# A new order of steps for a fused attention and gated-convolution kernel on one core

## The chip, the cores and the metric

The kernel runs on one core of one Trainium2 chip. The metric is device time in microseconds, from the first to the last instruction on the core as the host's runs report it; 2% is the smallest change that such runs are read for. A profiled execution gives the trace: each engine's instructions with their start, their length and what they waited for. The engines are PE (matrix products), DVE and ACT (elementwise work and copies out of the product banks), POOL and SP (here mostly issuing DMAs).

## The reference

Attention with 4 batches, 8 heads, 768 positions and 64 columns a head, in which each query sees 8 global keys and a local window of 96, with a bias that falls with distance. Its output, heads side by side (768 x 512), goes through a gated convolution over the sequence:

```python
scores = scale * np.matmul(q, k.transpose(0, 1, 3, 2))
is_global = pos[None, :] < int(n_global)
is_local = (rel >= 0) & (rel < int(n_local))
dist = np.where(is_global & ~is_local, float(n_local), np.abs(rel).astype(np.float32))
bias = -slopes[:, None, None] * dist[None, :, :]
scores = np.where(is_global | is_local, scores + bias[None, :, :, :], -1000000000.0)
a = softmax(scores)              # in the reference: max, exp, sum, written out
x = heads_side_by_side(a @ v)    # 4 x 768 x 512
proj = x @ w_proj                # 512 x 1536
x1, x2, x3 = (proj[..., :D], proj[..., D:2 * D], proj[..., 2 * D:])
X2 = np.fft.rfft(x2, n=S, axis=1)
H = np.fft.rfft(filter_fft, n=S, axis=0)[None, :, :]
x2_conv = np.fft.irfft(X2 * H, n=S, axis=1)
return ((x1 * x2_conv * x3) @ w_out).astype(np.float32)
```

All inputs and the output are float32 in DRAM; the kernel computes in float16 with float32 sums.

## The kernel before

The work is cut into 949 steps. A step is one to some sixteen instructions of one engine: a load, a group of score products into a bank, an exponential out of it, a product with the values, a division, a turn, a projection, a transform, an eviction, a store. Each batch has two stages. *Attention*: q and k are loaded, turned so that the 64 columns of a head lie along the partitions, multiplied (line 811, `scores`) key block by key block (seven blocks of 120 keys, with the 8 global keys ahead in each), exponentiated on ACT (line 823), masked on DVE (line 835), multiplied with v (lines 861 and 866) and divided by their sum (`xn`, line 885 in one DVE instruction for all heads, or line 889 in one small ACT instruction a head). *Convolution* (`conv`): x is turned (`xT`, line 913), projected with the 512 x 1536 weights (lines 988 to 993: gates; line 1049: the part that is convolved), transformed by products with cosine and sine tables after butterfly sums, multiplied with the filter's spectrum (lines 1216 to 1234), transformed back (lines 1136 to 1141), gated (lines 1191 to 1196) and multiplied with `w_out` (line 1100); an eviction into a buffer `ot` (line 318, one of six buffers) and a store of 256 KB (line 1107) follow. The attention of a batch overlaps the convolution of the one before.

The front does work of its own: tables of angles (a product of one-row tiles, lines 504 to 519), their sines by ACT, distances and masks (`dg`, `mask`), and idle products.

**What sets the order.** `ORDER` is a string of one word a step: `204P1` is step 204 on PE with product bank 1, `191A` step 191 on ACT. The letters are P (PE), A (ACT), V (DVE), G (POOL) and S (SP). `schedule` turns the string into the program, and each engine executes its words in this order; a step that can run on ACT or DVE goes where its letter says, and each step's inputs and buffers are guarded by semaphores between engines. The word `i1b0` is an idle product: one 128 x 512 product on a tile of zeros into bank 0, of which nothing is used (`busy`, line 310).

**How data comes in.** POOL issues 80 loads (line 330), DRAM to SBUF with a cast to float16, in the order of their words. A load waits until the one eight before it has landed. The first batch's q and k come as pairs of heads (`96x2x512`, four of each; one of each is loaded by SP), everything else by blocks of rows (`120x8x64` for k and v, `128x8x64` for q), the filter in one load of 768 KB (`g`), the projection's weights in slices (`w`). SP issues the copies of the global rows of k and v within SBUF (`kn<-kn`, `vn<-vn`), all stores, and, for the fourth batch alone, the turns by the crossbar (DMA_TRANSPOSE: q and k at line 773, x at line 900). The other batches are turned by products with the identity.

Of the kernel before, what the change touches and what calls it, by code (L numbers as in the profile page):

```python
# [43 lines left out]
204P1 22A 217V 38G 209P2 23V 26G 205A 219P0 39V 62V 63V i1b3 220A 52G 108P3 206V 210A 66P4 194A 207V 109A i1b5 27G  # L44
i1b5 211V 106P5 221V 42G 67V i1b1 i1b1 94P1 43G 212V 114P67 208A 110V 222V 92P4 213A 40G 95V i1b2 218A 111P23 223A
107A i1b0 41G 96V 64P0 93V i1b1 259G 115P 53V 224V 103P45 68V 65V 46G 195A 104P 112P 116A 80P1 199V 257G 9V 105A 81V
100P67 i1b0 i1b0 113A 101P 82V 225V 97P01 102A 6V 72P23 98P 232V 31A 73P 86P67 260G 99A 33S 117P45 226V 198V 74A 233V
78P0 118P 79A 75P23 234V 44G 76P 119A 32V 87P 235V 83P01 45G 77A i1b4 236V 69P45 256G 88A 70P 237V 84P 89P23 71A 258G
90P 238V 125P67 85A i1b4 227V 48G 126V 135P45 127V 91A 47G 120P01 136V 252P67 121V 267G 137V 130P23 253A 122V 241P4
254A 272G 138P5 131V 123P0 132V 249P67 266G 139V 352P1 251A 152P23 353V 273G 242A 133P7 250A 153V 157P45 268G 154V  # L50
124A 128P6 350P0 265G 158V 129A 155P1 159V 348P2 197A 354A 156A 49G 246P6 349V 160P4 351A 50G 244P5 134V 247A 161V
360P01 362P23 203V 271G 182V 361A 239P4 181V 140P67 274G 240A 175V 363A 174V 261G 143P01 177V 141A 202V 51G 245A
355P67 144V 275G 357P23 356A 377P5 375P4 176V 460G 358A 378V 414P6 165P01 184V 376A 264G 183V 415V 379A 277G 255V
380P45 385P67 381A 146P23 200V 185V 386A 178V 464G 142V 412P4 145V 186A 416P5 179V 162P67 476G 262S 180V 147A 417V
263S 413A 471G 148V 187V 387P23 418A 163A 149P45 359V 388A 243V 188V 289P6 270G 150A 189V 419P23 269G 290A 382P45 201V
279P7 151V 383A 389V 478G i1b6 420A 365P45 276G 281P6 166A 366V 367V 463G 280A 421P23 364V 426P01 282A 424P45 293P7
480G 422A 384V 283P6 425A 294V 461G 299P23 427A 167V 370P45 423V 477G 368P7 284A 171P01 369A 371V 472G 372V 300A
390P67 428V 462G 172A 395P45 164V 285P23 248A 469G 396V 173V 228P0 286A 391V 397V 291P1 470G 301V 229A 555P2 230A 392V
465G 434P45 292A 302V 231A 429P67 556A 468G 287V 168P01 430V 678G 557A 435V 431V 475G 551P2 436V 169A 373P3 553P6 664G
393P7 552A 374V 619P4 554V 398P5 295P01 394V 481G 620A 399V 580P2 288V 296A 563P45 663G 467S 565P67 581V 578P3 566A  # L60
466S 437P0 297V 667G 617P2 564A 170V 432P1 438V 686G 400P67 298V 618A 579V 682G 433A 309P2 567V 401A 681G 560P45
558P01 307P3 452V 310A 403P67 679G 561A 451V 685G 559A 305P2 402V 311P4 308A 453V 677G 303P5 404A 317P0 621V 454V
315P3 479G 306A 615P1 562V 406P67 318A 316A 670G 312A 616V 304A 455V 573P23 666G 407A 313P1 574V 405V 627P45 582A 456V
278G 314A 482P0 575V 628A 683G 408V 588P67 457V 483A 622P23 590P45 492P1 623A 474G 320V 319V 591A 409P23 665G 458V
493A 321V 674G 589A 459V 502P01 568P45 473G 322V 668S 503A 494P6 569V 323V 684G 410A 496P7 570V 495A 675G 324V 583P23
497A 624P45 592V 439P01 625A 676G 584A 504V 680G 585P45 626V 629P67 440A 571P2 484P3 673G 630A 411V 325V 498P01 586A
442P67 631V 762S 485A 326V 499A 486P3 760S 587V 443A 598P01 637P45 487A 599V 327V 761S 572A 445P67 600A 638V 639V 758S
488P23 441V 593P45 501V 489A 576P0 759S 333P1 328V 446A 632P23 594V 500V 334A 671S 595A 448P67 490V 669S 505V 784S
633V 336P1 444V 577A 634V 449A 640P4 601P0 491V 337A 768P23 596P5 641V 783S 769A 512P6 602V 508P7 597V 513A 765P01
509V 770P23 763P45 766A 786S 329V 635P6 506P7 771A 518P0 636V 510P1 785S 507V 764A 514P6 654V 606P23 511A 822S 519A  # L70
655V 515A 516P1 345P0 450V 517A 447V 821S 607A 772V 520P1 346A 794P67 787P23 608V 792P45 338S 521A 767V 342P0 793A
819S 656V 330P1 788A 522V 820S 778P45 343A 523V 603P23 331A 657V 795A 779V 658V 773P01 604A 612P67 332S 774V 780V 524A
672S 775V 339P4 613A 796V 828P01 340A 789P67 659V 825P23 605V 790A 341S 609P45 525V 829A 660V 526V 642P67 826A 781S
791V 4A 610A 823P23 776S 614V 830P01 3A 824A 611V 645P45 527V 831A 661V 782S 802P23 528V 643A 648P01 803V 529V 646A
335S 777S 804A 651P45 662V 644V 827V 797P67 649A 806S 700P2 798V 832V 799A 833P01 805S 647V 531V 689P3 701A 800S 702P6
834V 530V 690A 691P7 835V 703A 801S 652A 704P23 532V 838P01 692A 837S 705A 653V 693P67 839V 687P4 840V 694A 836S 698P5
706V 688A 695V 536P6 842S 699A 707V 709P45 696V 537A 533P7 841S 710A 708V 810P01 697V 534A 347S 711V 548P7 712V 811A
855V 721P6 719P0 722A 723P1 725P4 549A 856V 715P5 717P6 716A 727P2 550S 713P7 726A 545P3 344S 858V 720A 714A 857V
539P0 728A 718A 859V 542P2 724A 540A 860V 729V 875P1 546A 861V 547S 846P67 730V 862V 731A 864P3 863V 876A 732V 879P0
543A 865A 733V 544S 877P1 880A 538S 812V 734V 541S 886P23 878A 735V 868P0 887A 650V 738V 881P45 869A 866P1 882A 888V  # L80
816P23 736V 867A 883V 870P01 817A 807P45 889V 871A 884V 813P23 818V 808A 885V 847A 873V 911P4 892P5 809V 912A 896P0
872V 907P1 897A 849P67 893A 874V 908A 737V 814A 894P1 890P0 895A 905P5 739V 909P4 891A 843P23 906A 898V 910A 899V 914V
900A 852P45 913V 848V 915A 901V 815V 916V 749P0 853A 902V 917V 755P1 903V 750A 918V 844A 904V 751S 752P4 919V 535S
756A 854V 845V 740P5 933V 757S 850A 935V 746P1 753A 851V 934V 743P0 754S 747A 936V 741A 748S 943P1 920V 744A 742S
937P5 922V 944A 945S 921V 940P4 938A 745S 923V 939S 930P5 941V 942S 924P1 2A 931A 927P0 932S 925V 946P5 926S 928A 947A
929S 948S
"""


# [1292 lines left out]
```

## Time and profile before

| | us |
|---|---|
| median of three runs | 167.62 |
| the three runs | 166.46, 167.62, 171.16 |
| profiled execution, span from first to last instruction | 166.3 |
| PE busy, share | 157.9, 95% |
| DVE busy, share | 151.4, 91% |
| ACT busy, share | 148.2, 89% |
| POOL busy, share | 73.8, 44% |
| last step: product, eviction, store, end | from 162.25 |

Of the profiled execution only the span is given as its time; it lies 0.2 us under the fastest of the three runs. Three engines are busy for about nine tenths of the span, and they hand work to each other through eight product banks and a few buffers, so no single engine's sum tells the time: a wait on one shows as a gap on the next. Read the busy shares together with what ended each engine's idle time, and by stage: the front (up to some 20 us), the stretch in which loads still come in (to about 91 us), the stretch with turns by the crossbar, and the end.

### The profile page before, as it was taken

Reading aid. Unit: us, or ns where it says so; the run is one execution under the profiler, and the core shown is the slowest. Engines: PE = TensorE matmul, PEld = TensorE weight load, DVE = VectorE, ACT = ScalarE, POOL = GpSimd, SP = SyncE. Lnnn points to the kernel's source line nnn. Section 1 sums busy time; section 2 is a strip of 40 time slices with the busy share of each in tenths; the row PEclk is TensorE's granted clock in tenths of the full one; section 3 lists DMA queues with packets and bytes.
Section 4 is the critical chain, followed back from the end, with each engine's and each line's share of the span. In section 5 each row is a group of like instructions: output and inputs, shape, how many; then the busy total and the mean of one; then the engine's idle time right before and its main releaser. Section 6 shows DMA issues by size and latency. Waiting matters only on the chain.

```text
span 166.3 us, 4460 instructions
## 1 busy us (share of the span) xinstructions
PE 157.9 (95%) x1735; PEld 98.2 (59%) x1735; DVE 151.4 (91%) x348; ACT 148.2 (89%) x268; POOL 73.8 (44%) x94
## 2 busy tenths in 40 slices
PE   6999998999999999999999999999999699999991
PEld 2356566856536687765566685566555454585440
DVE  6898699899979999999999999999999979999960
ACT  3999995998999979999999999999997579998972
POOL 7896399999699979999730000000000000000000
PEclk9999999999999999999999999999999999999999
DMA  5999999999999999999999656423133135000696
GB/s 151 146 138 194 160 161 153 170 170 176 175 162 149 152 148 125 137 145 139 159 152 144 122 97 155 85 79 110 40 73 112 68 129 189 0 4 0 252 348 221
DMA packets 90365, 22.84 MB, mean 137 GB/s; under 512 B 81504, under 2 KB 87016, under 8 KB 90344
## 3 DMA queue, kind: packets, MB, share of 16 engines
q0 software_dynamic: 74880, 12.46, 100.9%
q1 hardware_dynamic: 15464, 10.10, 22.2%
q8 instruction: 13, 0.21, 0.5%
q14 instruction: 8, 0.07, 0.1%
HBM read 25.69 MB, written 6.29 MB: 192 GB/s over the span
## 4 chain that ended last, share of the span: by engine, by line
PE 50%; DMA 16%; DVE 15%; POOL 13%; issue 2%; SPq 1%; ACT 1%; ACTq 0%; POOLq 0%; DVEq 0%
PE bank L988 10%; PE bank L1100 10%; PE bank L1049 7%; DMA g<-in_moe_filter_fft_dram 6%; PE bank L990 5%; POOL kn L330 4%; DMA vn<-in_v_dram 4%; POOL qn L330 4%; DMA vn<-vn 3%; PE bank L811 3%; DVE xn L885 2%; DMA out_dram<-ot 2%; PE bank L861 2%; DVE E L835 2%; PE bank L866 2%
## 5 line engine op out<-in xcount | busy, mean ns | idle before, releaser
L823 ACT ACTIVATE E<-bank 128x864 f16<-128x864 f32 x48 | 40.5, 909 | 1.2 <-PE bank L811 1.1
L988 PE MATMUL bank<-xT,w 128*128 128x384 f16 x192 | 34.7, 326 | 0.0
L318 ACT ACTIVATE x<-bank 128x768 f16<-128x768 f32 (+2 forms) x31 | 25.5, 830 | 2.4 <-PE bank L988 1.0
L330 POOL DMA_DIRECT2D vn<-in_v_dram x28 | 25.6, 923 | 2.2 <-DMA w<-in_moe_w_proj_dram 1.6
L988 PEld LDWEIGHTS <-w 128*128 128x128 f16 x192 | 17.7, 98 | 11.1 <-issue 0.3
L1100 PE MATMUL bank<-wo,y 128*128 128x512 f16 (+1 forms) x100 | 22.5, 370 | 0.0
L330 POOL DMA_DIRECT2D kn<-in_k_dram x24 | 21.8, 910 | 1.5 <-DMA wo<-in_moe_w_out_dram 1.0
L330 POOL DMA_DIRECT2D qn<-in_q_dram x21 | 18.4, 881 | 5.7 <-DMA g<-in_moe_filter_fft_dram 4.2
L835 DVE TENSOR_TENSOR E<-E,mask 128x1728 f16<-128x1728 f16 x18 | 18.8, 1048 | 0.0
L318 ACT ACTIVATE ot<-bank 128x512 f32<-128x512 f32 (+1 forms) x23 | 12.9, 599 | 3.5 <-PE bank L1100 1.8
L885 DVE TENSOR_TENSOR xn<-bank,rc 128x512 f16<-128x512 f32 (+1 forms) x20 | 15.5, 789 | 0.3
L861 PEld LDWEIGHTS <-E 128*128 128x128 f16 x224 | 14.1, 97 | 2.8 <-DVE E L835 0.7
L1049 PE MATMUL bank<-w,xab 128*128 128x512 f16 x64 | 15.6, 379 | 0.0
L861 PE MATMUL bank<-vn,E 128*128 128x65 f16 x224 | 15.3, 193 | 0.2 <-DMA vn<-vn 0.2
L1100 PEld LDWEIGHTS <-y 128*128 128x128 f16 x100 | 9.5, 98 | 10.0 <-issue 0.3
L866 PE MATMUL bank<-vn,E 128*128 128x65 f16 x192 | 15.1, 193 | 0.0
L314 ACT CAST ab<-bank 128x512 f16<-128x512 f32 x23 | 13.7, 607 | 0.7 <-PE bank L1049 0.6
L866 PEld LDWEIGHTS <-E 128*128 128x128 f16 x192 | 13.2, 97 | 0.9
L811 PE MATMUL bank<-QT,KT 64*128 64x216 f16 (+2 forms) x224 | 13.3, 241 | 0.4 <-DVE pp L1229 0.4
L314 ACT CAST eo<-bank 128x384 f16<-128x384 f32 x30 | 12.9, 523 | 0.5 <-PE bank L1141 0.5
L314 ACT CAST X<-bank 128x1024 f16<-128x1024 f32 x12 | 12.2, 1032 | 0.0
L811 PEld LDWEIGHTS <-KT 64*128 64x128 f16 x224 | 7.9, 94 | 6.6 <-issue 5.2
(187 smaller groups left out, 363.0 us busy)
## 6 DMA issues: line engine op xcount, KB each, us to landing
out_dram<-ot SPq DMA_DIRECT2D x23, 256.0 KB
vn<-in_v_dram POOLq DMA_DIRECT2D x28, 120.0 KB, 6.1
kn<-in_k_dram POOLq DMA_DIRECT2D x21, 120.0 KB, 6.4
qn<-in_q_dram POOLq DMA_DIRECT2D x18, 128.0 KB, 6.1
w<-in_moe_w_proj_dram POOLq DMA_DIRECT2D x4, 256.0 KB, 6.8
g<-in_moe_filter_fft_dram POOLq DMA_DIRECT2D x1, 768.0 KB, 10.6
kn<-in_k_dram POOLq DMA_DIRECT2D x3, 192.0 KB, 4.3
qn<-in_q_dram POOLq DMA_DIRECT2D x3, 192.0 KB, 5.0
```

The costliest lines, as they stand in the source:

```text
L314: {"A": nc.scalar.copy, "V": nc.vector.tensor_copy, "G": nc.gpsimd.tensor_copy}[e](out, in_)
L318: self.nc.scalar.mul(out, in_, c)
L330: return self.g.op(eng, 0.57 + 0.00035 * nbytes[0] if eng == "G" else 0.5, lambda _: e.dma_start(dst, src), w=w, r=r, nbytes=nbytes, name= ...
L811: nc.tensor.matmul(bs[hh].f32()[:, off:off + w], self.KT[hs, hp, P * m:P * m + P], self.QT[hs, hp, KL * m:KL * m + w], start=(off == 0 and ...
L823: g.op("A", act(864), lambda _: nc.scalar.activation(eo, bs[0].two()[:, :, 0:432].rearrange("p h (m w) -> p h m w", m=2), Act.Exp, scale=s ...
L835: g.op("V", dve(1728, 2), lambda _: nc.vector.tensor_mul(ep, ep, mk), r=[("mask", h) for h in range(hs.start, hs.stop)] + ([("mask0", hp - ...
L861: nc.tensor.matmul(o[:, n, hh], ef[:, at:at + P], vt[:, t, 2 * hp + hh, 0:D + 1], start=first, stop=(t == 0), skip_group_check=True)
L866: nc.tensor.matmul(o[:, n, hh], ef[:, at:at + P], vt[:, t - 1, 2 * hp + hh, 0:D + 1], start=False, stop=True, skip_group_check=True)
L885: nc.vector.tensor_mul(to, o[:, :, :, 0:D], rc.to_broadcast([P, 2, 2 * nt, D]))
L988: nc.tensor.matmul(bk.f32()[:, 0:h], w, self.xT[:, c, lo:lo + h], **kw)
L1049: nc.tensor.matmul(bk.f32(), src[:, c], w[:, c, DM:2 * DM], start=(c == 0), stop=(c == 3))
L1100: nc.tensor.matmul(bk.f32()[:, 0:n], y[:, c, P * t:P * t + P], self.wo[:, c, ns], start=(c == 0), stop=(c == 3))
```

## The change

The string `ORDER` is another one; nothing else in the file differs. It holds the same 949 steps, 18 idle products instead of 26, other banks, and for 48 steps the other one of ACT and DVE. It is one line shorter, so line numbers in the new file are smaller by one. Its first lines, and one from the middle:

```diff
-0V 34G 18S 30S i1b0 15V i1b0 21S 5G 35V i1b0 60V i1b0 59V 57V 10G 55V 7V i1b0 14V i1b0 24G 1V 56V 191A 8V i1b0 17V 61A
-28G 190A i1b0 12A 20V i1b0 36V i1b0 19A 54V 58V 37G 214P0 13V 193A i1b1 29G 11V 215A i1b1 16V 192A i1b1 196A 25G 216V
...
+18S 0V 15V 36V 6V 7V 14A 5G 21S 12A 25G 8V i1b0 i1b0 i1b0 i1b0 219P0 220A 221V 204P1 222V 24G 205A 28G 209P2 210A 211V
+10G 61V 27G 214P3 215A 29G 16V 30S 26G 34G 52G 206V 207V 223A 216V 23A i1b4 i1b4 i1b4 i1b4 i1b4 64P0 i1b4 i1b4 66P1
...
+782S 341S 831A 651P23 660V 833P67 829A 648P45 347S 524V 776S 644V 525V 647V 806S 652A 526V 800S 661V 834V 687P2 835A
```

**PE, front.** Before, ten idle products stand ahead of the first product of the angle tables (steps 214, 204, 209, 219), and the other sixteen follow one to three at a time, up to the values of the second batch. Now four stand ahead of the four angle steps and five behind them, then come the first turns of q and k (steps 64 and 66) with two idle products between them, and the last seven follow ahead of step 111.

**POOL, front.** POOL's queue from its first own instructions to the first loads of v: `dg` is the distance table, `eo` a spare buffer with the rows for the angle tables, `ident` the identity, `g_85` the filter, `96x2x512` a pair of heads of the first batch. Before:

```order
L549 IOTA dg 128x216
L551 AFFINE_SELECT dg<-dg 128x216 x2
L403 IOTA eo 1x512
L405 IOTA eo 1x128
masks.py:197 MEMSET ident 128x128
masks.py:199 AFFINE_SELECT ident<-ident 128x128
L330 DMA kn<-in_k_dram 96x2x512 x2
L568 AFFINE_SELECT eo<-eo 8x120 x2
L330 DMA qn<-in_q_dram 96x2x512 x2
L571 AFFINE_SELECT tail<-tail 128x1
L330 DMA kn<-in_k_dram 96x2x512
L330 DMA g_85<-in_moe_filter_fft_dram 128x6x512
```

Now:

```order
L402 IOTA eo 1x512
L404 IOTA eo 1x128
L329 DMA qn<-in_q_dram 96x2x512
L329 DMA kn<-in_k_dram 96x2x512 x2
masks.py:197 MEMSET ident 128x128
masks.py:199 AFFINE_SELECT ident<-ident 128x128
L329 DMA qn<-in_q_dram 96x2x512 x2
L329 DMA kn<-in_k_dram 96x2x512
L548 IOTA dg 128x216
L550 AFFINE_SELECT dg<-dg 128x216 x2
L329 DMA g_85<-in_moe_filter_fft_dram 128x6x512
```

The distance table moved from first place to just ahead of the filter, three loads moved ahead of the identity, and all six pair loads are ahead of the filter, which is the seventh load and not the sixth. Behind it, blocks of q and k of the second batch now come ahead of the first v blocks, and the weight slices are later: the one from column 1280 is the 31st load and was the 29th.

**ACT, front.** From ACT's first instructions: `mask` is the exponential of the distance table, `E` and `y` belong to the angle tables, `ab` and `identb` are casts. Before:

```order
L314 CAST identb<-ident 128x128
L612 ACTIVATE mask<-dg 128x216
L447 COPY E<-eo 128x2x6x32
L448 ACTIVATE E<-eo 128x2x80
L314 CAST ab_87<-ot 96x512
```

Now:

```order
L446 COPY E<-eo 128x2x6x32
L447 ACTIVATE E<-eo 128x2x80
L460 ACTIVATE y<-bank_104 128x256
L460 ACTIVATE y<-bank_104 128x512
L460 ACTIVATE y<-bank_105 128x256 x2
L474 ACT_TABLE_LOAD
L474 ACTIVATE p_81<-y 128x256
```

The work on the angle tables moved ahead of the masks; six of the eight masks now stand between the first batch's score exponentials or behind them, where seven stood ahead of these.

**SP, from the end of q's and k's turns.** SP's queue, stores (`out_dram<-ot`) and turns of x (`xT<-xn`, with two or three blocks each). Before:

```order
L1107 DMA out_dram<-ot 128x512
L900 DMA_TRANSPOSE xT<-xn_70 128x2x128
L900 DMA_TRANSPOSE xT<-xn_69 128x2x128
L900 DMA_TRANSPOSE xT<-xn_70 128x2x128
L1107 DMA out_dram<-ot 128x512
L900 DMA_TRANSPOSE xT<-xn_69 128x2x128
L900 DMA_TRANSPOSE xT<-xn_70 128x2x128 x2
L900 DMA_TRANSPOSE xT<-xn_69 128x2x128 x2
L900 DMA_TRANSPOSE xT<-xn_69 128x3x128 x2
L900 DMA_TRANSPOSE xT<-xn_70 128x3x128 x2
L1107 DMA out_dram<-ot 128x512 x13
```

Now:

```order
L1106 DMA out_dram<-ot 128x512
L899 DMA_TRANSPOSE xT<-xn_69 128x2x128
L899 DMA_TRANSPOSE xT<-xn_70 128x2x128
L1106 DMA out_dram<-ot 128x512 x2
L899 DMA_TRANSPOSE xT<-xn_69 128x2x128
L899 DMA_TRANSPOSE xT<-xn_70 128x2x128
L899 DMA_TRANSPOSE xT<-xn_69 128x2x128 x2
L899 DMA_TRANSPOSE xT<-xn_70 128x2x128
L899 DMA_TRANSPOSE xT<-xn_69 128x3x128 x2
L899 DMA_TRANSPOSE xT<-xn_70 128x3x128 x2
L1106 DMA out_dram<-ot 128x512 x14
```

Two stores (steps 341 and 347) now stand together ahead of the last nine turns; before, one (step 335) stood there, and step 347 was the first behind the turns. Steps 332 and 335 are now behind them. Farther ahead in SP's queue, the thirteen turns of the fourth batch's q and k start with step 759, right behind the last score products of the third batch (step 588), and stand closer together; before, they started with step 762, some ten microseconds of PE's work later.

More of the change, by code (lines that the diff above doesn't have):

```diff
@@ L47 @@
[L47 to L81, printed above, removed]
@@ new lines @@
+104P 198V 83P45 274G 49G 105A 232V 9V 99A 233V 234V 226V 50G 117P01 84P 118P 235V 227V 85A 86P23 87P 88A 75P67 76P
+348P4 236V 261G 119A 125P23 350P5 89P01 237V 77A 351A 349V 352P4 238V 270G 196A 126V 127V 199V 264G 120P67 121V 197A
+353V 135P23 239P5 90P 240A 136V 122V 244P4 91A 462G 130P67 241P5 354V 242A 137V 357P01 157P23 131V 224V 123P5 358A
+245V 464G 51G 132V 138P4 152P67 195A 194A 158V 159V 355P01 269G 460G 153V 124A 200V 139A 133P5 160P2 201V 128P4 1V
+134A 463G 246P3 377P5 154V 356A 161V 129A 362P67 360P01 378V 361A 471G 182V 181V 247A 184V 17V 263S 363A 155P2 461G
@@ new lines @@
+575V 311P0 307P1 316A 309P4 590P67 588P23 312A 308A 676G 453V 591A 313P5 409P01 759S 405V 629P67 454V 455V 587V 589A
+624P23 314A 758S 492P5 310A 303P4 625A 410A 406P23 456V 304A 576P4 493A 682G 482P5 407A 562V 457V 442P23 411V 458V
+762S 577A 568P01 626V 592V 459V 675G 681G 483A 569V 630A 631V 443A 502P45 503A 598P67 683G 599V 760S 484P2 444V 637P45
+680G 570A 486P3 278G 786S 600V 571P0 632P67 485A 319V 408V 761S 487A 593P23 638V 320V 572A 639V 488P01 321A 439P45
+594V 633V 489A 785S 595V 634V 763P23 322V 440A 783S 764A 768P01 504V 784S 769A 448P67 449A 494P2 640P3 673G 765P01
@@ L87 @@
+854V 901V 849P23 749P0 916V 902V 917V 746P1 753A 903V 918V 756A 904V 850A 919V 851V 740P2 935V 750A 747A 933V 754S
+936V 934V 743P3 946P1 920V 757S 741A 922V 943P2 947V 940P0 751S 937P1 921V 748S 742S 744A 745S 944A 945S 948S 941A
+938A 942S 2A 939S 923V 924P0 925V 927P1 928V 926S 929S 930P2 931A 932S
 """
```

36 lines of the change are left out of this document (28 added, 8 removed).

## The prediction

> **What bounds the kernel now.** I read the page's first part, then the busy time by stage, then the waits of each engine, then the chain that ended last.
>
> ```profile
> span 166.3 us, 4460 instructions
> PE 157.9 (95%) x1735; PEld 98.2 (59%) x1735; DVE 151.4 (91%) x348; ACT 148.2 (89%) x268; POOL 73.8 (44%) x94
> ...
> 0.00:20.00 20.00, 18.23 (x216) 9.08 (x217) 15.56 (x72) 17.22 (x33) 14.43 (x28) 1.00 1.12 158
> 20.00:50.00 30.00, 28.98 (x381) 19.05 (x377) 28.05 (x67) 26.70 (x44) 27.27 (x32) 1.00 2.10 166
> 50.00:98.00 48.00, 47.61 (x618) 33.04 (x615) 46.91 (x91) 46.51 (x86) 32.13 (x36) 1.00 1.97 141
> 98.00:130.00 32.00, 31.98 (x320) 19.65 (x318) 31.83 (x60) 29.51 (x58) 0.00 (x0) 1.00 0.37 91
> 130.00:163.00 33.00, 31.09 (x219) 17.33 (x217) 29.01 (x64) 28.15 (x51) 0.00 (x0) 1.00 0.36 133
> ```
>
> The columns after a stretch's length are PE, PEld, DVE, ACT and POOL. PE is busy 95% of the span, but the five rows show that nothing there is bound by PE alone: between 20 and 130 us DVE and ACT run with hardly more room, and PE's idle time lies in the front (20 - 18.23 = 1.8 us up to 20, 1.0 up to 50) and after 130 us (1.9 us). ACT's idle time up to 98 us is 2.8 + 3.3 + 1.5 = 7.6 us; I need that sum below.
>
> The second thing to see is that "busy" is not "useful" in the front. The idle products (line 310, products on a tile of zeros that no result uses) fill it:
>
> ```profile
> L310 PE MATMUL bank<-eo x26: 377/390/634, 1.3 to 47.9; 128*128 128x512 f16 x26
> 1.26 4.45 PE L310 MATMUL bank<-eo 128*128 128x512 f16 x10 [1.26 <-DVE eo L396]
> 5.64 0.39 PE L504 MATMUL bank<-eo 1*128 1x128 f16 x2
> ```
>
> Ten of them stand before the first useful product, which starts at 5.64 us; (5.64 - 1.26) / 10 is 0.44 us each. What waits for what:
>
> ```profile
> POOL qn L330 <- DMA g<-in_moe_filter_fft_dram: 4.2, 1, 4.2
> ACT L612 <- DVE dg L557: 2.5, 1, 2.5
> ACT h L318 <- PE bank L690: 2.0, 2, 1.3
> ACT ot L318 <- DMA out_dram<-ot: 1.7, 1, 1.7
> POOL vn L330 <- DMA w<-in_moe_w_proj_dram: 1.6, 2, 1.3
> PE bank L1139 <- ACT ot L318: 1.5, 1, 1.5
> ...
> 8.27 10.61 DMA g<-in_moe_filter_fft_dram
> 35.60 7.14 DMA vn<-in_v_dram
> 42.76 5.62 DMA vn<-vn
> 48.52 0.22 PE bank L861 x2
> 94.51 0.36 PE bank L811 x4
> ...
> 125.68 1.25 SPq L900
> 126.98 3.91 DMA out_dram<-ot
> 130.91 0.61 ACT ot L318
> 131.56 0.27 PE bank L1139 x2
> 152.19 9.98 PE bank L1100 x48
> 162.25 0.60 ACT ot L318
> ```
>
> The upper rows are waits (sum, times, longest), the lower ones pieces of the chain (start, length). Two places carry the time. First, the loads: POOL issues them in order, and the eighth load behind the 768 KB filter stands until that has landed (18.9 us); everything that POOL issues later is late by that, and the chain runs through POOL's loads into a v load at 35.6 and a copy of its global rows at 42.76, for which PE waits until 48.5. Second, at 131 us: an ACT eviction into an `ot` buffer waits for an old output store, and PE waits 1.5 us for that eviction's bank. The store sat in SP's queue behind turns by the crossbar:
>
> ```profile
> 83.71 1.66 SPq L773 DMA_TRANSPOSE KT<-kn  x1
> 114.30 12.63 SPq L900 DMA_TRANSPOSE xT<-xn  x9
> 126.98 36.72 SPq L1107 DMA_DIRECT2D out_dram<-ot  x21
> ```
>
> From 152 us on the last output products follow one another, and 166.3 - 162.25 = 4.0 us are eviction, store and end.
>
> **The change, part by part.** It is the same 949 steps and 18 idle products for 26, in another order on every engine, so I price places, not instructions.
>
> *Idle products and the front.* Four stand before the angle products for ten: 6 x 0.44 = 2.6 us earlier on PE there. Eight fewer in all are worth at most 6 x 0.44 + 2 x 0.22 = 3.1 us. What hides that gain is the load stream, so I take it from there:
>
> ```profile
> 19.41 0.90 POOL L330 DMA_DIRECT2D qn<-in_q_dram  x1 [4.23 <-DMA g<-in_moe_filter_fft_dram]
> 31.93 1.54 POOL L330 DMA_DIRECT2D w<-in_moe_w_proj_dram  x2
> w<-in_moe_w_proj_dram POOLq DMA_DIRECT2D x4, 256.0 KB, 6.8
> 40.86 1.48 PE L988 MATMUL bank<-xT,w 128*128 128x384 f16 x8
> ```
>
> Before, the filter is POOL's sixth load and the 14th (at 19.41 us) waits for it; now it is the seventh and the 15th waits. It goes out at about the same 8 us, as POOL's other front work is the same (0.9 us a load), but the pair loads ahead of it leave from about 1.7 us and not 3.4, so it should land up to 1.2 us earlier. One more load stands ahead of the wait (0.9 us). So load number n past the 15th is some 2.0 us earlier. But the numbers changed: the weight slice from column 1280 (the second of the two issued from 31.93 us, landing at 33.47 + 6.8 = 40.3), behind which the product at 40.86 us starts, is the 31st and not the 29th, 2 x 0.9 = 1.8 us back. That leaves 0.2 us there, and up to 0.6 more because the wait at 48.5 us (the global rows of v, now asked for well ahead of their product) goes. I take -0.5 at 50 us; the ends are 0 and -2.6, all of the idle products before the angles.
>
> *ACT.* 48 steps change between ACT and DVE, among them these:
>
> ```profile
> L314 ACT COPY xT<-bank 128x480 f16<-128x480 f16 x5 | 3.0, 605 | 0.4 <-PE bank L913 0.3
> L889 ACT ACTIVATE xn<-bank,rc 128x64 f16<-128x64 f32 x32 | 7.1, 375 | 0.0
> ```
>
> Six `xT` copies move to ACT (6 x 0.6 = 3.6 us), and 36 of the small `xn` products for 32 (7.1 / 32 = 0.22 each, 0.9 us); casts, query and key copies, evictions and gate sums go both ways and give back some 1.5. ACT has about 3.0 us more, 2.5 of it before the last score products (about 98 us). It had 7.6 us idle up to there. If the new order leaves 5.1 idle, ACT is even with before; with 4.5, 0.6 earlier; if no idle time is filled, 2.5 later. What goes is part of the 2.5 us at its start, as its first work no longer needs the distance table (the page row of line 612), and part of the 2.0 us of `h` waits, which follow the filter. Against it: the first exponential comes behind more small copies. So I expect ACT idle at 4.5 to 5.5 and the time at 98 us moved by -0.2 (ends -2.6 and +2.5): the later of the load path and ACT decides, and the -0.5 is not kept whole.
>
> *An old store before the turns.* The store of step 347, for whose buffer ACT waits until 130.9, stood behind all twelve turns of x and now stands ahead of the last nine; steps 332 and 335 go behind the turns for it, whose buffers are asked for 5 to 9 us of PE work later. ACT's 1.7 us at 129 go, and with them PE's 1.5. What is late next is the last turn of x, which DVE's butterflies take: four stores stand ahead of it in either order, so it is issued no later than at 125.68. I take -1.3 (ends 0 and -1.7).
>
> *The turns of the fourth batch's q and k.* They move from behind the last loads (83.71 us) to about 72 us (they wait for the last score products of the third batch), beside the last dozen loads. Before, PE waited for no turn, and few ran beside loads. The nearest rows:
>
> ```profile
> SPq L773 <- DMA kn<-kn: 4.8, 1, 4.8
> 78.10 0.69 SPq L330 DMA_DIRECT2D kn<-kn  x1
> q0 software_dynamic: 28180, 3.86, 177.7%
> L935 DVE TENSOR_TENSOR xab<-xT x2: 751/752/752, 128.2 to 129.2; 128x1152 f16<-128x1152 f16 x2
> ```
>
> A copy of 16 KB issued at 78.1 us beside loads landed at 83.6: 5.5 us. The last turn of x, with no loads about, was issued at 125.68 and used at 128.2: 2.5 us. The third row is the loads' queue between 60 and 95 us: its packets fill 1.8 times what the engines have. The first scores that need the turns began at 94.5; counting PE's rows between both places they now stand 7 us of PE work earlier, near 87 us. With an issue every 1.2 us and 5.5 us each, the sixth turn, the last that they need, is there by 72 + 6 x 1.2 + 5.5 = 84.7. I take 0, by the row of the copy. The ends: 0, and +5 if the turns land only once the loads are drained and slow these too.
>
> The Trainium skill ("DMA: Bandwidth & Descriptors", section "Queues, rings and completion order") says each DMA engine goes round between the queue rows that have work, a packet at a time. By that a turn beside loads takes about twice its time alone and costs the sum nothing; the 5.5 us copy above is that with little to spare.
>
> *Tail.* The last product is now a whole 512-column group with its 256 KB store: +0.2 us, inside the 4.0 us of the tail (ends 0 and +0.5).
>
> *Sum.* 166.3 - 0.2 - 1.3 + 0.2 = 165.0 us of span. The runs of before lie at 166.46, 167.62 (median) and 171.16, 0.2 to 4.9 above the profiled span; with 0.5 for that I predict **165.5 us**.
>
> **The rivals.**
> *The front's gain carries through.* ACT's 7.6 us of idle time are enough for its new work, DVE and ACT being 91% and 89% busy with room in the front. Then 2.0 to 2.6 us of the front and 1.5 of the store come off: 166.3 - 2.3 - 1.5 + 0.2 + 0.5 = 163.2. Against it: the weights come only 0.2 us earlier.
> *ACT takes the gain and more.* ACT idle up to 98 us does not fall below 7.0, so +1.9 there, the store gives -1.3: 166.3 + 1.9 - 1.3 + 0.2 + 0.5 = 167.6. For it: ACT is the engine that got work; against: its idle time at the start is a wait on work that now comes later.
> *The turns come late* (the slower side). They and the loads share 16 engines that are already full. From the point where the sixth turn lands after 87 us, PE waits at the first scores of batch 3 for each microsecond; if the loads of that batch are slowed as well, POOL, whose next load waits for the eighth before it, holds the k rows of later turns too. 3 to 6 us with the rest as forecast: 165.5 + 4.5 = 170.
> *The clock comes later.* The profile prints full clock in every slice, yet products of 512 columns are spaced 0.44 us up to 5.7 us and 9.98 / 48 = 0.21 at the end; the ten idle products cover that time. The new front has four and then angle products with one row, and gaps. If the faster spacing comes 3 us later, some 3 us of work takes twice as long, at most +1.5: 167.0. The Trainium skill ("TensorE: Matmul & The Clock Gate", section "Part 1: The HAM clock gate") gives a free-running window of about 3.4 us in which the array must be busy. By that rule a gap in the front could cost one window more, the 1.5 us above; the trace's change of spacing near 5.7 us agrees with it and does not show what counts as busy.
>
> **How the numbers follow.** Forecast 0.48 (164.3 to 166.6), front gain whole 0.17 (162.5 to 164.3), ACT 0.15 (166.6 to 168.6), late turns 0.15 (168 to 172), clock 0.05. The range that leaves out 2 in 10 is 162.8 to 169.8. Runs of this kernel differ by some 2% (166.5 to 171.2), so 2% is about what can be told from no change: from 167.62, under 164.3 is faster, above 171.0 slower. Faster: 0.17 and the low end of the forecast, 0.22. Slower: half of the late turns, and what 48 changed engines may hold that I did not price, 0.15. Within: 0.63.
>
> **What would show it.** First angle product near 3.2 us, four idle products before it; the wait of POOL behind the filter ending near 18 us; no wait of PE for global rows of v near 48; ACT idle up to 98 us near 5; no ACT wait for an output store at 129; no PE wait over 0.5 us at the first scores of the fourth batch (near 87 us). The prediction is wrong if that last one shows microseconds, if ACT's idle time stays at 7, or if the products' spacing stays at 0.44 us beyond 7 us.

## The result

The changed kernel took 173.01 us (median of four runs, 171.20 to 174.22) against 167.04 us before (165.84 to 171.16, four runs): 1.040 times the time, 95% interval 1.028 to 1.051. Ratios in this document compare means of runs in the faster of two states, here 172.41 us (the changed kernel without its run of 174.22) with 165.84 (the run of before made beside them), so 1.040 is not the quotient of the medians, which is 1.036. The change is slower by about 6 us, and outside the forecast range of 162.8 to 169.8. A run's time lies 1.7 us above its span. The profiled execution (172.5 us, mean granted clock 0.980) is the slowest of the four; the others have spans of 169.5 to 172.0 and mean clocks of 0.979 to 0.989. That fits the half clock shown below but does not show it for them, as twenty runs of the kernel before have mean clocks of 0.966 to 1.00.

The page of the changed kernel: busy times, then strips of 40 slices of 4.3 us.

```profile
span 172.5 us, 4461 instructions
PE 160.9 (93%) x1727; PEld 98.8 (57%) x1727; DVE 151.4 (88%) x346; ACT 151.1 (88%) x274; POOL 74.0 (43%) x94
...
PE   7999999999999999999907999999999999999891
...
DVE  4778999989999999999990389999999999999961
ACT  7999997999999999999913599999989899989661
...
PEclk9999999999999999999995699999999999999999
```

One hole stands in the middle of every compute engine, in slices 21 to 23 (86 to 99 us): PE and ACT first, DVE a slice later. The clock strip drops behind PE's hole. Apart from that the strips are as full as before.

The same by stage, with the hole in stages of its own (the columns are start and end, length, then busy time of PE, PEld, DVE, ACT and POOL, granted clock, DMA share and GB/s):

```profile
0.00:20.00 20.00, 18.55 (x211) 9.01 (x212) 14.58 (x65) 18.51 (x35) 17.10 (x31) 1.00 1.35 179
20.00:50.00 30.00, 29.64 (x386) 20.03 (x385) 28.87 (x72) 28.16 (x45) 27.55 (x32) 1.00 2.12 165
50.00:84.00 34.00, 34.00 (x470) 23.77 (x469) 33.79 (x65) 33.53 (x66) 29.33 (x33) 1.00 2.12 144
84.00:90.50 6.50, 2.40 (x32) 1.38 (x28) 6.25 (x11) 3.08 (x4) 0.00 (x0) 1.00 1.84 108
90.50:97.50 7.00, 5.74 (x26) 2.81 (x26) 1.24 (x4) 2.90 (x4) 0.00 (x0) 0.52 1.72 150
```

The stretch from 50 to 98 us of the kernel before, in two stages:

```profile
50.00:84.00 34.00, 34.00 (x428) 23.21 (x425) 33.46 (x65) 32.86 (x54) 31.60 (x36) 1.00 2.12 145
84.00:98.00 14.00, 13.61 (x192) 9.84 (x191) 13.46 (x27) 13.65 (x33) 0.54 (x1) 1.00 1.62 131
```

Up to 84 us the engines of the new order are idle for less time than those of the old: ACT for 1.5 + 1.8 + 0.5 = 3.8 us, where it was 2.8 + 3.3 + 1.1 = 7.2. Then PE works 2.4 of 6.5 us, and in the 7 us behind that the clock is at 0.52, so PE's 5.7 busy us do about half the work.

The waits name the cause, in sum, times and longest; behind them the rows of PE and SP at the place, and the DMAs issued from 72.5 to 101 us with the size of each and the median time from issue to landing:

```profile
DVE g L979 <- ACT x L317: 5.8, 1, 5.8
PEld L810 <- DMA KT<-kn: 5.7, 1, 5.7
ACT E L822 <- PE bank L810: 5.6, 2, 5.0
PE bank L810 <- DMA KT<-kn: 5.4, 1, 5.4
...
84.93 1.46 PE L987 MATMUL bank<-xT,w 128*128 128x384 f16 x8
91.76 0.90 PE L810 MATMUL bank<-QT,KT 64*128 64x216 f16 x8 [5.36 <-DMA KT<-kn]
...
72.25 3.00 SPq L772 DMA_TRANSPOSE QT<-qn  x2
82.28 4.42 SPq L772 DMA_TRANSPOSE KT<-kn  x2
91.87 4.97 SPq L772 DMA_TRANSPOSE KT<-kn  x3
...
vn<-in_v_dram POOLq DMA_DIRECT2D x7, 120.0 KB, 17.0
wo<-in_moe_w_out_dram POOLq DMA_DIRECT2D x1, 512.0 KB, 9.8
```

The v loads of before, issued in the same stretch of its time:

```profile
vn<-in_v_dram POOLq DMA_DIRECT2D x4, 120.0 KB, 7.7
```

PE is ready for the first scores of the fourth batch at 86.4 us and gets them at 91.76, when a turn of k lands, the sixth, issued at 82.28: 9.4 us from issue to landing. By the trace the first seven of these turns took 9.4 to 11.4 us each; turns of q and k that ran without loads took 2.4 to 2.5 in before. ACT waits for these scores and DVE for ACT. The thirteen turns are issued from 72.25 to 96.84 us, one every 2.0 us up to the sixth and 1.9 us each over all, where one took 1.2 to 1.3 before. The last seven v loads, which run beside them, take 17.0 us to land, for 7.7 before. It looks as if turns and loads slowed one another; the runs below test it. The 1.7 us of ACT at 129, for an old store, are gone.

### The profile page after: what moved, and what is told of

The parts are those of the page before. It is cut to its first block, busy times and chain, and to the rows that moved or that the text cites. A ratio compares the mean times of both kernels' runs of the same rounds, so it can differ in the third digit from the quotient of the medians.

```text
span 172.5 us, 4461 instructions
## 1 busy us (share of the span) xinstructions
PE 160.9 (93%) x1727; PEld 98.8 (57%) x1727; DVE 151.4 (88%) x346; ACT 151.1 (88%) x274; POOL 74.0 (43%) x94
## 5 line engine op out<-in xcount | busy, mean ns | idle before, releaser
L987 PE MATMUL bank<-xT,w 128*128 128x384 f16 x192 | 35.8, 334 | 0.1
L329 POOL DMA_DIRECT2D vn<-in_v_dram x28 | 26.1, 967 | 0.1
L987 PEld LDWEIGHTS <-w 128*128 128x128 f16 x192 | 18.2, 99 | 12.8 <-issue 1.7
L329 POOL DMA_DIRECT2D kn<-in_k_dram x24 | 22.3, 943 | 4.1 <-DMA w<-in_moe_w_proj_dram 2.0
L810 PE MATMUL bank<-QT,KT 64*128 64x216 f16 (+2 forms) x224 | 14.3, 246 | 5.5 <-DMA KT<-kn 5.4
L329 POOL DMA_DIRECT2D qn<-in_q_dram x21 | 19.1, 916 | 0.2
L1048 PE MATMUL bank<-w,xab 128*128 128x512 f16 x64 | 16.7, 395 | 0.0
L979 DVE TENSOR_TENSOR g<-x 128x384 f16<-128x384 f16 (+2 forms) x32 | 10.9, 346 | 5.8 <-ACT x L317 5.8
L313 ACT CAST ab<-bank 128x512 f16<-128x512 f32 x21 | 12.3, 605 | 2.1 <-PE bank L1048 2.0
```

Source lines behind the costliest of these rows:

```text
L313: {"A": nc.scalar.copy, "V": nc.vector.tensor_copy, "G": nc.gpsimd.tensor_copy}[e](out, in_)
L329: return self.g.op(eng, 0.57 + 0.00035 * nbytes[0] if eng == "G" else 0.5, lambda _: e.dma_start(dst, src), w=w, r=r, nbytes=nbytes, name= ...
L810: nc.tensor.matmul(bs[hh].f32()[:, off:off + w], self.KT[hs, hp, P * m:P * m + P], self.QT[hs, hp, KL * m:KL * m + w], start=(off == 0 and ...
L987: nc.tensor.matmul(bk.f32()[:, 0:h], w, self.xT[:, c, lo:lo + h], **kw)
L1048: nc.tensor.matmul(bk.f32(), src[:, c], w[:, c, DM:2 * DM], start=(c == 0), stop=(c == 3))
```

## The experiments

The theory after this reading: the turns of the fourth batch's q and k beside the last loads land late; PE waits 5.4 us, and the half clock behind the wait costs some 3 us more; the rest of the order is about as good as before. The main rivals: turns are slow by themselves; the time went elsewhere in the order; the later clock in the front costs it. Where an edit changes `ORDER`, a diff shows only the pieces of its lines around the edit, with `...` between places.

**Without the loads beside the turns.** The seven v loads of the fourth batch are left out:

```diff
         for t in ts:
-            self.load_rows(("vn", s), vt, self.v, b, t)
+            if b == 3:
+                self.loads += 1
+                self.g.op("G", 0.9, lambda _: None, w=[("vn", s, t)], name="left out", bias=-2000.0 + self.loads)
+            else:
+                self.load_rows(("vn", s), vt, self.v, b, t)
```

> The changed kernel without the seven loads of the fourth batch's v (the last seven of POOL's 80 loads; the second batch's rows of v stay in the buffer, so the fourth batch's output is not the reference's). Theory A (the turns of the fourth batch's q and k and these loads slow one another, and the first scores of that batch wait for the turns): the sixth turn lands by 86 us instead of 91.6, PE's wait of 5.4 us at line 810 falls under 1 us, the half clock from 90.7 to 97 us goes with it, and the time falls by 7 to 8.5 us to about 165. Theory B (turns are slow by themselves when SP issues them one behind the other; the loads do not matter): the turns still land 1.6 us apart, the wait stays above 4 us and the time above 171. Theory C (the time was lost elsewhere in the new order): the wait may go, but the time stays above 169.

It took 167.11 us (ten runs), 1.002 times before (0.996 to 1.008). The wait is gone and the clock stays; PE goes from the gate products straight to the scores:

```profile
87.19 1.47 PE L991 MATMUL bank<-xT,w 128*128 128x384 f16 x8
88.58 0.55 PE L814 MATMUL bank<-QT,KT 64*128 64x216 f16 x8
```

Without these loads 5.9 us come off, so theories B and C fall, by the wait and by the time: the loads beside the turns cost nearly all that the change costs. Some details are not as expected. The sixth turn, issued at 83.41, landed at 87.28 and not by 86 (3.9 us, for 9.4); the first turns, still beside the 512 KB load of `w_out`, took 9.2 us, and the issues were still 1.6 us apart, the sign named for theory B. And PE asked for the turn only at 88.58, 2.2 us later than in the changed kernel's profile, since in this execution the full clock came later in the front (14.5 us, for 8.9); had it asked at 86.4, it would have waited about 0.9 us, not 5.4. The time that came off is less than the 7 to 8.5 expected: without the wait the new order equals the old one and no more, though it also carries seven loads less.

**What the wait does to the clock.** 24 idle products ahead of the first scores:

```diff
-594V 633V 489A 785S 595V 634V 763P23
+594V 633V 489A 785S 595V 634V i24b2 763P23
```

> The changed kernel with 24 idle products ahead of the first scores of the fourth batch (24 x 0.216 = 5.2 us), where PE waits 5.4 us for a turn. Theory A says that this place costs twice: 5.4 us of waiting, and then about 3 us because the granted clock is at half for some 6 us behind it. With PE busy in the wait the clock stays at 1.0 and the time falls by 2.5 to 3.5 us, the scores still starting near 91.7. If the clock drop were an effect of something else (a throttle by load), it stays at 0.5 to 0.7 in that stretch and the time does not change by more than 0.5.

171.72 us (four runs, 1.027 times before). PE's rows and two stages of it:

```profile
86.43 5.34 PE L309 MATMUL bank<-eo 128*128 128x512 f16 x24
91.71 0.55 PE L810 MATMUL bank<-QT,KT 64*128 64x216 f16 x8
...
84.00:90.50 6.50, 6.50 (x58) 3.53 (x55) 2.67 (x6) 3.27 (x5) 0.00 (x0) 1.00 1.86 128
90.50:97.50 7.00, 7.00 (x60) 4.05 (x59) 5.55 (x11) 5.16 (x7) 0.00 (x0) 1.00 1.77 114
```

The scores start at 91.71, as in the changed kernel, and the clock stays at 1.00. So the half clock is an effect of the idle PE. What it costs is less sure: the medians differ by 1.3 us, the profiled executions by 2.5 (170.0 for 172.5), and without the changed kernel's run of 174.22 the means differ by 0.5 (171.87 for 172.41). The runs of the two kernels overlap, so a cost of about 1.3 us is an estimate that is not clear of noise, and below the 2.5 to 3.5 expected. The wait itself is the larger part.

**A 512 KB load out of the turns' way.** The load of `w_out` left POOL with the first turn. Moved ahead of the fourth batch's first k load:

```diff
-371V 249P67 289P0 555P1 189V 390P23 372V 250A 290V 173V 251A 365P45 666G 556A
+371V 249P67 289P0 555P1 189V 390P23 372V 250A 290V 173V 251A 365P45 278G 666G 556A
...
-680G 570A 486P3 278G 786S 600V
+680G 570A 486P3 786S 600V
```

> The changed kernel with one word moved: the 512 KB load of w_out (72nd of 80, issued at 72.1 us together with the first turn, landed at 81.8 as did that turn) now ahead of the first k load of the fourth batch (53rd, issued near 54). Same DMA work, same first turn at 72 us. Theory A1 (the turns get their share of the engines by packets, and a load with 2 KB packets takes most of it): the first turn lands by 78 us instead of 81.8, the sixth by 88 instead of 91.6, PE's wait at the first scores of the fourth batch falls from 5.4 to 0 to 2 us, without a clock drop; time 166.5 to 169 for 173. Rival A0 (any load counts alike, the sum of bytes sets when the turns are through): the sixth turn still lands after 90.5, the time moves by less than 1 us.

169.51 us, 1.016 times before (1.004 to 1.028), 3.5 us under the changed kernel. The wait at the scores, and the stage behind:

```profile
88.64 0.55 PE L810 MATMUL bank<-QT,KT 64*128 64x216 f16 x8 [2.30 <-DMA KT<-kn]
...
90.50:97.50 7.00, 7.00 (x65) 4.06 (x64) 5.06 (x11) 6.76 (x11) 0.00 (x0) 1.00 1.49 130
...
vn<-in_v_dram POOLq DMA_DIRECT2D x7, 120.0 KB, 13.3
...
78.05 4.69 SPq L772 DMA_TRANSPOSE KT<-kn  x3
```

5.4 us of wait became 2.3, and after 2.3 us the clock does not drop. One word, not on PE, ACT or DVE, gives back more than half of the loss. All figures of A1 are missed by a little (first turn landed at 79.2 us, sixth at 88.6, wait 2.3, time 169.5), those of A0 by much. What gained is the issue: the first six turns were issued 1.45 us apart and not 2.0, so the sixth went out at 79.42 us (the second of the last row) and not at 82.28. The sixth itself still took 9.2 us to land. The texts on record speak of packets of 2 KB; by the trace this load has rows of 2 KB and moves as 512 packets of 1,024 B, beside packets of 128 B of the v loads and 256 B of the turns.

**The same load behind all others.** Is it that this load's rows are long, or that there is more to transfer?

```diff
-680G 570A 486P3 278G 786S 600V
+680G 570A 486P3 673G 670G 679G 678G 686G 685G 684G 278G 786S 600V
```

> The changed kernel with the load of w_out behind the seven last v loads (80th and last, issued near 78.5 us and not 72.1), so that the first turns run beside small-packet loads alone and the same work is in the queues by 80 us. It tells apart why the earlier w_out let the turns land sooner. Theory A1 (a load whose rows are 2 KB long takes the engines from turns whose packets are small): the first turns land by 79 us, the wait at the first scores of the fourth batch falls from 5.4 to 3 us or less, as with the earlier load. Theory A0 (only the amount of transfers still ahead counts): the sixth turn lands near 91 again and the wait stays above 4 us. In either case the output products that need w_out can wait for it near 95 us, so the time is not compared.

In the profiled execution (173.5 us) the wait at the first scores stayed, though the v loads landed fast again:

```profile
92.31 0.90 PE L810 MATMUL bank<-QT,KT 64*128 64x216 f16 x8 [5.25 <-DMA KT<-kn]
...
vn<-in_v_dram POOLq DMA_DIRECT2D x7, 120.0 KB, 7.1
wo<-in_moe_w_out_dram POOLq DMA_DIRECT2D x1, 512.0 KB, 13.7
```

By the trace the first turn landed at 79.1 us, for 82.1 in the changed kernel, about as A1 had it; the sixth took 12.0 us and landed at 92.3, with the load itself at 92.1, as A0 had it. Neither theory holds whole. What the three profiles show is that the wait is shorter, though not gone, when this load has gone ahead of the turns. Whether by its size or its row length stays open. The four runs took 169.2 to 173.5 us (median 171.94); two of them, 169.2 and 170.6, have a mean clock of 0.997, so the wait and the half clock of the profile are not shown for these.

**The store, alone, in the kernel before.**

```diff
-335S 777S 804A 651P45
+335S 347S 777S 804A 651P45
...
-697V 534A 347S 711V
+697V 534A 711V
```

> The kernel before with one word moved: the store of step 347 directly behind that of step 335, ahead of nine turns of x, not behind them. My prediction's term: ACT's wait of 1.7 us for that store at 129 and PE's of 1.5 behind it go, the nine turns are issued 0.5 us later, and the span falls by 1.0 to 1.5 us from 166.3. Rival: the last turn of x, 0.5 us later, is what DVE's butterflies then wait for, and less than 0.5 us comes off.

0.999 times before (0.993 to 1.005): nothing came off. In its profile ACT does not wait for the store, but DVE waits for the last turn of x:

```profile
DVE xab L935 <- DMA xT<-xn: 2.0, 1, 2.0
126.21 3.89 DMA xT<-xn
```

That turn took 3.9 us, where the last turn of x took 2.5 in the profile of before; and in the profile of before it is the store that took 3.91 us. In a third profile with before's store order, that of the kernel before with an early `w_out` (below), neither is waited for. What the two slow landings share is one packet of another queue, which the profile calls "instruction", between 124 and 132 us. First in before, then in this run:

```profile
q8 instruction: 1, 0.02, 1.0%
...
q8 instruction: 1, 0.02, 0.7%
```

By the trace this packet of 16 KB was under way from 128.17 to 129.45 us in before, and from 128.08 to 129.00 here. The trace holds sixteen completions of each of these transfers; fifteen of the store's were there by 129.23 and the last at 130.89, fifteen of the turn's by 128.60 and the last at 130.10. The fourteen traces together have 168 turns of x. In 35 of them such a packet ran, and 29 of these took 2.8 to 4.3 us; the other 139 turns, 133 of them without such a packet, took 2.3 to 2.5. So the queue's order is not what made the landing at 129 late by some 1.6 us: whichever of the two was under way there was late. This is read off the traces; no run moved the packets.

**The front and the clock.** In the texts on record A1 is the theory on the load of `w_out` from above, A2 that the ten idle products are what opens the clock. The kernel before with four idle products ahead of the angle products:

```diff
-18S 30S i1b0 15V i1b0 21S 5G 35V i1b0 60V i1b0 59V 57V 10G 55V 7V i1b0 14V i1b0 24G 1V 56V 191A 8V i1b0 17V 61A
-28G 190A i1b0 12A 20V i1b0 36V i1b0 19A 54V 58V 37G 214P0
+18S 30S i1b0 15V i1b0 21S 5G 35V i1b0 60V i1b0 59V 57V 10G 55V 7V 14V 24G 1V 56V 191A 8V 17V 61A
+28G 190A 12A 20V 36V 19A 54V 58V 37G 214P0
```

> The kernel before with four idle products ahead of the first angle products and not ten (20 in all), nothing else. Theory A2: the full clock comes later than 7 us (8 to 14), as in the changed kernel, and the time rises by 0.5 to 3 us. Rival: the clock comes near 6 us all the same, the angle products start up to 2.6 us earlier, and the time is the same or up to 0.5 us less (the loads decide).

1.008 times before (1.003 to 1.014): 1.4 us slower. Groups of sixteen turning products of one shape show the clock in that kernel, 0.85 us at half and 0.53 at full:

```profile
13.04 0.85 PE L741 MATMUL bank<-ident,kn 96*64 96x96 f16 x16
16.26 0.53 PE L741 MATMUL bank<-ident,qn 96*64 96x96 f16 x16
```

The full clock came at 15.0 us, for 5.9 before. And the changed kernel with ten idle products there:

```diff
-25G 8V i1b0 i1b0 i1b0 i1b0 219P0 220A 221V 204P1
+25G 8V i1b0 i1b0 i1b0 i1b0 i1b0 i1b0 i1b0 i1b0 i1b0 i1b0 219P0 220A 221V 204P1
```

> The changed kernel with six more idle products ahead of the angle products (ten, as before; 24 in all). In the changed kernel the full clock was granted at 8.9 us in one profile and at 14.5 us in the profile of the kernel without the last v loads, whose front is the same; before it was 5.9. Theory A2 (the idle products open the clock gate, and angle products with one row do not count): grant at 6 to 7 us again, first angle product at 5.6, and PE at 28 us no later than in the changed kernel; the time moves by -0.5 to -2 us (from 173), since the later part keeps its wait for turns. Rival (the ten idle products only fill a wait): grant still after 8.5 us, and the time the same or up to 2.5 us more.

176.07 us, 3 us slower than the changed kernel: both the expectation (0.5 to 2 us less) and its rival (up to 2.5 more, with a late clock) are missed. The clock came early, at 4.4 us, as the first row shows (a product of 256 columns in 0.28 us, 0.39 in the changed kernel), but what follows waits for the angles:

```profile
5.07 0.28 PE L509 MATMUL bank<-eo 1*128 1x256 f16 x1
DVE y L463 <- ACT y L460: 3.1, 1, 3.1
ACT y L460 <- PE bank L510: 1.8, 1, 1.8
```

The theory that the new front lacks idle products falls for the changed kernel: its first steps need the angle products at 3.1 us, two us earlier, and what that delay costs is more than the earlier clock gives. In before's front, where the angles are not next, the same six products are worth 1.4 us.

**Mends together, and joined orders.** The early `w_out`, a turn that the first scores do not need behind the last that they do (step 786 behind 761), and ten idle products:

> The changed kernel with three edits: the load of w_out moved as in the run before last, the turn of step 786, which the first scores do not need, behind that of step 761, which they do, and ten idle products ahead of the angle products. Theory A1 with A2: the fifth turn, now the last needed, lands 1.6 us earlier than with the moved load alone, no wait at the first scores over 0.5 us, grant near 6 to 7 us; time 164 to 166.5, at or under before (167.4). Theory A0: still above 169.

170.22 us, 1.019 times before, for at most 166.5 expected. The wait is down to 0.84 us, but the scores start at 89.71 us, later than the 88.64 of the early load alone, as the ten idle products put the front back here too. So the time above 169, named as the sign of A0, does not speak for it. With steps 448, 494 and 640 ahead of the first scores in place of the idle products:

> The changed kernel with the load of w_out moved ahead of the fourth batch's k (which took PE's wait from 5.4 to 2.3 us), the turn of step 786 behind that of 761 (the last one that the first scores need is then the fifth, some 1.2 us earlier), and the steps 448, 494 and 640 on PE (about 2 us of its work) ahead of the first scores instead of right behind them. Theory: 2.3 us of wait minus 1.2 minus 2 leaves none; span 164 to 165, time 165.5 to 167, at or up to 1% under before (167.4). Rival: ACT and DVE, who wait for these scores, run dry, and what PE does not wait comes off less than half: 167 to 168.5.

169.67 us, 1.020 times before (1.010 to 1.029), above the expected 165.5 to 167 and above the rival's 168.5. PE no longer waits for turns, but four score steps stand in a row and wait for their banks:

```profile
PE bank L810 <- ACT E L822: 2.0, 2, 1.0
```

The edit also put the first of these steps on banks 0 and 1 for 2 and 3 (763P01 for 763P23), which the steps 768 and 765 behind it use too, so the bank waits come in part from that.

Two joined orders, first the changed kernel up to step 443 and before behind it, then before up to step 595 and the changed kernel behind it:

> The changed kernel's order up to step 443 (some 6 us of PE's work before the first scores of the fourth batch, two turns already issued), then the order of before for all steps that are left; one product bank differs. The first scores of the fourth batch come again behind as much PE work as before (some 7 us more). Theory A: the turns land as late as in the changed kernel (sixth near 91 to 92) but are asked for at about 93, so PE waits under 1 us, the clock stays, and the span is that of before less the 0.4 us by which the new front is ahead there: 165 to 166.5, with the 1.5 us wait for an old store at about 130 back. Theory C (the front or the engine assignment lost the time): above 168.

> The order of before up to step 595 (where the first scores of the fourth batch come next), then the changed kernel's order for all steps that are left; no bank differs. In the traces the part behind 100 us costs PE 3.2 us above its useful work in before and 1 to 2 in the changed kernel, whose order has no wait for an old store. Theory: front and turns as before, no stall at 129, 1 to 1.5 us less than before: ratio 0.990 to 0.995. Rival: the second part was only free of that wait because the wait for turns ahead of it gave ACT, DVE and SP time to catch up; then the ratio is 0.998 to 1.005.

172.19 us (1.027 times before) and 176.46 us (1.059): both far above what was expected, and neither tells the theories apart: 172.19 is above the 168 named for theory C, but the seam explains it. The rows below are PE at its longest wait and a stage of the first, then a wait of the second. In the first one the turns are not waited for; a gate step waits 3.1 us for DVE's division, as DVE's queue was made for another place, and half clock follows. In the second, scores wait 3.9 us for turns in three pieces, which the first part, the order of before, starts late, and half clock stands behind them too. The seam made new waits.

```profile
86.11 2.72 PE L987 MATMUL bank<-xT,w 128*128 128x384 f16 x8 [3.13 <-DVE xn L884]
84.00:90.50 6.50, 4.39 (x16) 2.15 (x16) 4.82 (x9) 0.81 (x1) 0.00 (x0) 0.60 1.67 128
...
PE bank L811 <- DMA QT<-qn: 3.9, 3, 1.8
```

**The early `w_out` in the kernel before.** The word 278G moved ahead of 666G there too:

> The kernel before with the same word moved as in the run on the changed kernel: w_out ahead of the first k load of the fourth batch (70th load in before). There the turns are not waited for, so if the theory (that load hurts by what it does to turns that PE waits for) holds, the time stays within 0.5% of before. Rival: an earlier w_out is good for the stream by itself: 1% or more off here too.

0.999 times before (0.994 to 1.004), as expected: the load hurts where PE waits for turns, and before does not. None of the twelve kernels is faster than before by more than its interval.

## Why the prediction was wrong, point by point

- *The turns*: the step that failed. "I take 0, by the row of the copy": I let a 16 KB copy within SBUF, issued at 78.1, stand for a turn of 128 x 512 beside the 512 KB load and seven more. The sixth turn was to land at 84.7; by PE's row it landed at 91.7. Of these 7 us, 3.1 are the issue (82.28 for the sum's 72 + 6 x 1.2 = 79.2): beside the loads a turn was issued every 2.0 us and not every 1.2. The other 3.9 are the landing, 9.4 us by the trace where the copy took 5.5. (Between the first turn and the sixth lie five intervals, so the sum's own terms give 83.5.) Nearer rows than the copy stood in the trace of before, and I passed them over: three turns issued at 83.71, 85.55 and 86.85, beside the last loads, took 7.5, 5.9 and 5.0 us to land. With 7.5 the sum gives 86.7, and no slack is left before 87.
- *The rival of the late turns* named this wait, with a chance of 0.15 and the bound "+5 if the turns land only once the loads are drained and slow these too". Its time was too low as well: 173.0 lies above its 168 to 172, and its second half, late k rows, did not come: the last k load landed at 75.2 us.
- From the rule of the Trainium skill that I set beside it ("DMA: Bandwidth & Descriptors", section "Queues, rings and completion order": an engine goes round between the queue rows that have work, a packet at a time) I estimated that a turn beside loads takes about twice its time alone, so 5 us for 2.5. Measured: 9.4. That the engines go round between queues is not contradicted, since turns landed among the loads; the factor of two was mine and does not follow from it.
- *The clock behind a stall* was in no term: about 1.3 us by the medians of the run with the busy wait, not clear of noise (0.5 to 2.5). I priced the clock in the front alone.
- *The store*, -1.3: wrong, about 0 by its own run. ACT's wait stood in the trace, but not because of the store's place in the queue: what was under way at that time landed some 1.6 us late, first the store and, with the store moved, the last turn.
- *ACT*: right in kind, better than forecast. Idle up to 84 us is 3.8 us (50 to 84 us: 0.5, before 1.1), where I looked for about 5 up to 98. Behind 84 us the wait for the turn covers the rest of this sign.
- *The front*: the first angle product starts at 3.08 us (forecast 3.2); no POOL wait names the filter any more, and PE's idle time up to 50 us is 1.8 us for 2.8. The full clock came at 8.9 us, so the sign that I named for the rival of the late clock (half clock beyond 7 us) was there; the run with ten idle products shows that it was not what this order lacked, while in the kernel before the same edit costs 1.4 us, near that rival's 1.5.
- *Time above the span*: I took 0.5 us; it is 1.7 in every run. So the profiled execution of before, 166.3 us of span, is one of about 168.0 us, and not one just under the fastest run.

The sum, for the profiled executions: 172.5 - 166.3 = 6.2. The wait is 5.4 and the half clock about 1.3, so the rest of the order, front, ACT and store together, is worth -0.5 there (-1.7 if the half clock costs 2.5); by the medians (173.0, 167.1 without the wait, 167.0 before) it is worth about nothing.

## What to carry to other kernels

Where a transfer is moved beside others, look in the trace for a transfer of the same kind that already runs beside some, and not for another kind of the same size: here turns of 5.0 to 7.5 us were there to be read. Take the bad end seriously, and ask first how much earlier the result is now needed: here 7 us of PE's work less were left, and 5.4 were missing. A wait on PE can cost twice, once as the wait and once as half clock behind it: here half clock followed one of 3.1 us, and two of 1 us close together, but not one of 2.3 us. And ask of a late landing what else ran at that time before its place in the order is blamed.

## What the runs showed of the hardware

- Turns by the crossbar and loads through POOL slow each other. The turn that PE waits for took 9.4 us beside loads, and turns of its kind 2.4 to 2.5 alone; turns were issued 2.0 us apart beside loads, 1.2 to 1.3 alone. The v loads took 17.0 us beside turns and the 512 KB load, 13.3 with that load gone ahead, 7.1 when it came last, and 7.7 in before.
- An idle PE of 5.4 us was followed by half clock from 90.8 to 97.6 us, one of 3.1 us (the first joined order) by half clock from 85.2 to 92.1; one of 2.3 us (the early load) by none. Shorter waits close together had it too: 0.98, 0.98 and 0.16 us between 90.0 and 93.0 (three steps moved), half clock from 92.3 to 95.7. It does not follow the length of the wait alone: behind 5.25 us (the load behind all others) it lasted from 92.1 to 95.5 only. The Trainium skill ("TensorE: Matmul & The Clock Gate", section "Part 1: The HAM clock gate") gives windows of about 3.4 us; the half clocks here lasted one or two of these, and less than one window of idle time was enough.
- The full clock in the front came between 4.0 and 6.8 us in the six profiles with ten 128 x 512 products at the start, and between 8.6 and 15.0 in the eight with four and then products of one row. The changed kernel and its variants with the same front had it at 8.6, 8.9, 9.1, 10.1, 10.2, 10.3 and 14.5 us: one order, seven times.
- A packet of 16 KB of the queue that the profile calls "instruction" mostly came with a late landing of the DMA under way: of 35 turns of x with such a packet in their time, 29 took 2.8 to 4.3 us, and without one 133 took 2.3 to 2.5.
